# Large loads on GpSimd's queue, and other numbers for the scheduler, in a gated scan followed by an MLP

## The chip, the cores and the metric

One core of a Trainium2 chip (trn2). The metric is the device time of one execution in microseconds. Five engines run their own instruction streams in order: TensorE (PE, with its weight loads as PEld), VectorE (DVE), ScalarE (ACT), GpSimd (POOL) and SyncE (SP). Data transfers are issued from an engine's queue, also in order: a transfer whose input or buffer is not ready holds up what stands behind it.

## The reference

For each of 4 batches and 8 heads, a complex gated state of 48 x 48 is carried over 768 steps; its real part, read out by q, gives rows of 384 per token, which go through an MLP with a piecewise activation.

```python
scale = np.minimum(mag, 0.999) / (mag + 1e-06)
a_re_n, a_im_n = (a_re * scale, a_im * scale)
for t in range(S):
    new_re = ar * S_re - ai * S_im
    new_im = ar * S_im + ai * S_re
    S_re, S_im = (new_re + kv, new_im)          # kv = k[t] outer v[t]
    y[:, :, t] = np.einsum('bhd,bhde->bhe', q[:, :, t], S_re)
...
h = x @ w_in                                    # 3072 x 384 by 384 x 2048
g = np.where(h >= 1, h, np.where(h <= -1, 0.0, (h + 1) ** 2 / 4))
return g @ w_out
```

a_re and a_im are drawn 8 times larger than the setup's own draw.

## The kernel before

**Tiling.** The 3072 tokens are 12 units of 256; two units make a block, so there are six blocks of 512 columns. Unit u is unit 0 or 1 of its block u // 2. The scan is not stepped: a unit's gates become running sums of log-magnitude and angle, and the read-out becomes masked products of k and q within chunks of 128 tokens plus a carried state.

**A unit's work.** `gates(u)` loads ai (both parts of a), kq and V, works on ScalarE (Ln, Exp, Arctan, Sin, Abs; helper line L597) and VectorE (L611, L615, L625, L635, scans L695 and L745, L760, L766, L714), and ends with two products of 1536 columns (L823). Their rows are then re-arranged over partitions into hd by ten transfers, the *spreads* (`spread`; issued through the helper at L390, shown as hd<-x and hd<-kq). `attend(u)` is a series of short TensorE visits: sc (scores, L978), tp (transposes, L922), yp (L1019, L1027) and dp (state, L951), with VectorE's mask products am (L986) and ScalarE's copies into xr (L1039). After the second yp of a unit six small transfers, the *moves* (xr<-xr, 16 KB each), bring rows of two heads to their places. The second chunk's yp_1_0 of a unit is its last for the moves.

**A block's work.** `moe(blk)` first splits xr into xH (ScalarE, L1118) and xL (VectorE, L1125), one slice of 128 rows at a time for the second unit. Then for each of 16 slices f of the hidden layer: nine products h (L1148; two with xH and one with xL for each of three row slices), the activation, and nine products o (L1223), three slices later. h has two PSUM banks. The activation is s (ScalarE, L1173), g (VectorE, L1192), gh (ScalarE, L1206) and gl (VectorE, L1210). Blocks below SPARE take two further steps on ScalarE (L1183, L1187), the others one on VectorE (L1200). Results are copied by ScalarE (L1250) and stored; those copies share three buffers with s and g of the next block.

**Weights** arrive in 16 loads of 768 KB (`load`, L405), two buffers in turn after the first four, and are decoded on VectorE (L420, L429, L438, L449) and ScalarE (L444) during the start and block 0. Some of the decoding of the first four is done by TensorE ("rest"). In the last block the weights are loaded again for range checks (chk, `ranges`); `bounds` checks ai of the first four units (chk_ai, L523 to L547).

**What sets the order.** Every step is given to `Plan.op` with an engine, an assumed duration, what it reads and writes, and for some a due time; `Plan.order` is a list scheduler that walks through assumed time and writes one order per engine. Due times come from FIRST (the assumed start of block 0), the blocks' assumed durations DUR, and for visits from windows (HEAD, EARLY, WINDOW). A transfer costs its queue DMA_ISSUE and ends DMA_FIX plus its bytes over a rate (LOAD or MOVE) later. HOLD and QUEUE let an engine or SyncE wait for a more urgent step that comes soon. On the chip only the orders and the true dependences are left: nothing waits for an assumed time. All transfers stand on SyncE's queue; GpSimd has nothing to do after its constants. Idle TensorE products (L1278) are put into gaps of the assumed schedule before block 0.

Of the kernel before, what the change touches and what calls it, by code (L numbers as in the profile page):

```python
# [12 lines left out]
U32 = mybir.dt.uint32  # L13
# [5 lines left out]
P = 128  # L19
# [5 lines left out]
DM = NH * D  # L25
# [7 lines left out]
NC = U // CH  # L33
# [23 lines left out]
LAT = {"PE": 260, "DVE": 190, "ACT": 190, "SP": 0, "POOL": 200}  # L57
SAME = {"PE": 0, "DVE": 122, "ACT": 128, "SP": 0, "POOL": 0}
TOKEN = (("o2", "at2"), ("o2", "o0"))
DMA_FIX, DMA_END, DMA_ISSUE, LANES = 2400, 50, 470, 8  # L60
LOAD, MOVE = 410.0, 240.0
LATE = 2000
LATE_MOVE = 0
TABLE = 1294
FIRST = 51000
SLACK = 1.04
LAG = 3
SPREADS = 0
SPREAD = ("SP", "ACT")
HOLD = {'DVE': (2, 2000.0), 'ACT': (2, 2000.0)}  # L70
QUEUE = (0.3, 0.0)
WINDOW = (0.0, 0.7)
EARLY = (0.15, 0.9)
HEAD = ((30000, 15000), (25000, 2000))
HOME = 4
SPARE = 2
LEAD = 8000
WARM = 0.85
BRIDGE = 4
ABS_ACT = 5  # L80
LO_PE = 4
INFLATE = 1.6
SPLIT_DUE = 3000
# [215 lines left out]


def per(n):
    return n / 2.4 + 14


def moe_time(n):
# [14 lines left out]
def gated_scan_moe(  # L320
    ctx: ExitStack, tc: tile.TileContext, kq, ari, art, v, wl, qn, kn, arn, ain, vn, out
):
    nc = tc.nc
# [61 lines left out]
    def dma(nbytes, dst, src, r=(), w=(), due=None, rate=LOAD, eng="SP", after=(), late=0):  # L385
        queue = {"SP": nc.sync, "ACT": nc.scalar, "POOL": nc.gpsimd}[eng]
        return pl.op(
            eng,
            DMA_ISSUE,
            lambda: queue.dma_start(dst(), src()),  # L390
            r=r,
            w=w,
            dma=nbytes / rate,
            due=due,
            after=after,
            late=late,
        )
# [3 lines left out]

    def load(k, raw):
        nc.sync.dma_start(raw.rearrange("p n t -> p (n t)"), wl[k].bitcast(U32))  # L405

    def weights(n, kind, i, slot):
        k = i + (NF // 2 if kind == "o" else 0)
        RAW = tl(slot, [P, 2 * DM, 2], U32, f"raw_{kind}{i}")
        Y = tl("y", [P, 2 * DM], U32, f"y_{kind}{i}")  # L410
        W = weight[kind, i] = tl(f"w{kind}{i}", [P, 2, 2, DM], F32R, f"w{kind}_{i}")
        hi, lo = (lambda: W.get()[:, :, 0]), (lambda: W.get()[:, :, 1])
        wide = lambda t: t.rearrange("p (e n) -> p e n", e=2)
        top, low = (lambda: RAW.get()[:, :, 1]), (lambda: RAW.get()[:, :, 0])
        N = 2 * DM
        pl.op("SP", DMA_ISSUE, lambda: load(k, RAW.get()), w=[RAW], dma=P * N * 8 / LOAD, late=LATE if n > 2 else 0)
# [18 lines left out]
        pl.op(  # L435
            "DVE",
            dve(N),
            lambda: V_.scalar_tensor_tensor(  # L438
                low(), top(), 0xC0000000, low(), op0=ALU.bitwise_and, op1=ALU.bitwise_or
            ),  # L440
            w=[(RAW, 0)],
        )
        yf = lambda: wide(low().bitcast(F32))
        pl.op("ACT", act(N) + 50, lambda: A_.copy(hi(), yf()), r=[(RAW, 0)], w=[(W, 0)])  # L444
        if n >= LO_PE:
            pl.op(
                "DVE",
                dve(N),
                lambda: V_.tensor_tensor(lo(), yf(), hi().bitcast(F32), op=ALU.subtract),  # L449
                r=[(RAW, 0), (W, 0)],  # L450
                w=[(W, 1)],
            )
# [60 lines left out]
    def bounds(u):  # L513
# [5 lines left out]
        dma(P * 2 * N * 4, lambda: AI.get(), lambda: ari[PLACE[u]], w=[AI], late=LATE)  # L519
        pl.op(  # L520
            "DVE",
            dve(N, True),
# [35 lines left out]
    def gates(u):  # L558
# [21 lines left out]
        if u == 0:  # L580
            for e in range(2):
                dma(
                    size,
                    lambda e=e: AI.get()[:, e],
                    lambda e=e: art[u, :, e],
                    w=[(AI, e)],
                )
        else:
            dma(2 * size, lambda: AI.get(), lambda: (art[u] if by_token else ari[place]), w=[a, i], after=moved if u == 3 else (), late=LATE if u > 2 else 0)

        def ac(out, src, f, r, w, tab=False, **kw):
            acc_ = kw.get("accum_out")
# [117 lines left out]
            ac(X1, X0, AF.Exp, [x0], [x1], True, scale=-1.0)  # L710
            ac(X0, X0, AF.Exp, [], [x0], True)

        dma(2 * size, lambda: KQ.get(), lambda: kq[place], w=[KQ], after=moved if u == 2 else (), late=LATE if u > 1 else 0)
        ve(dve(2 * N), lambda: V_.tensor_tensor(KQ.get(), KQ.get(), X.get(), op=ALU.mult), [X], [KQ])  # L714

        yield
# [81 lines left out]
            )  # L798
        else:
            vt[u] = tl("V0", [P, NC, DM], F32, f"V_{u}")  # L800
        dma(P * NC * DM * 4, lambda t=vt[u]: t.get(), lambda: v[place], w=[vt[u]], late=LATE if u > 1 else 0)
        if u == 1:
            hd = [
                guest(
# [82 lines left out]
    def attend(u):  # L887
# [112 lines left out]
        def values(c, ams, st):  # L1000
# [64 lines left out]
        def visit(parts):  # L1065
            reads = [x for p in parts for x in p[2]]
            last = None
            for n, (cost, run, r, psum, tail) in enumerate(parts):
                cost += 90 if n == len(parts) - 1 else 0
                last = pl.op("PE", cost, run, r=reads if n == 0 else r, w=[psum], glue=last)  # L1070
                visits.append((len(todo_visits), last))
                kinds[last] = "att"
                tail()
            todo_visits.append(0)
# [493 lines left out]
```

## Time and profile before

| | |
|---|---|
| median of 3 runs | 582.93 us (582.11 to 583.48) |
| the profiled execution | 585.01 us |
| its span, first to last instruction | 583.2 us |
| mean granted TensorE clock | 0.992 |
| first product h of block 0 | 71.2 us into the span |
| last product o | ends at about 575.8 us |
| transfers | 77.42 MB, all but 0.72 MB of it on one queue |

The profile shows an engine's instructions with start and length in microseconds from the start of the span, and in brackets how long it was idle before and what ended that. SPq is the issue of a transfer; its landing comes later. A row of the chain of waits ("DMA xr<-xr") is the time in which the chain waited for that transfer. In a group's row stand the count, the busy us and mean ns, and the idle us before it. Line numbers are those of the kernel before.

### The profile page before, as it was taken

The page shows a single profiled execution, that of the slowest core. Times are in us where ns is not written, and L with a number is a line of the kernel's source. Part 1 is how long each engine was busy: PE and PEld are TensorE (multiplying, and loading weights), DVE is VectorE, ACT ScalarE, POOL GpSimd, SP SyncE. Part 2 cuts the span into 40 slices and gives each one's busy share as a digit, 9 for nine tenths or more (in the row PEclk, how much of TensorE's full clock was granted, in tenths as well). Part 3 has the DMA queues.
Part 4 walks back from the last instruction along what each step waited for, and adds up shares of the span by engine and source line. Part 5 has one row for each costly group of instructions (what it writes and reads, how often), then busy time and mean ns, then how long its engine had stood idle before and what let it go on. Part 6 is the DMA issues. An engine that isn't in the chain of part 4 may idle for free.

```text
span 583.2 us, 9954 instructions
## 1 busy us (share of the span) xinstructions
PE 565.9 (97%) x3908; PEld 477.9 (82%) x3908; DVE 431.9 (74%) x624; ACT 407.0 (70%) x656; POOL 1.7 (0%) x20
## 2 busy tenths in 40 slices
PE   8999999999999999999999999999999999999995
PEld 8788888888788888877888888888888888888883
DVE  4999999999769398469599778797875544455452
ACT  7777799887798899886475666756643322369972
POOL 1000000000000000000000000000000000000000
PEclk9999999999989999999999999999999999999998
DMA  8686551854640721740711521601511400078711
GB/s 353 242 224 215 173 190 63 249 210 148 164 157 0 205 101 55 177 182 12 189 52 36 187 85 53 198 1 51 148 55 31 112 1 4 12 263 310 267 72 61
DMA packets 23527, 77.42 MB, mean 133 GB/s; under 512 B 4528, under 2 KB 10288, under 8 KB 23472
## 3 DMA queue, kind: packets, MB, share of 16 engines
q1 hardware_dynamic: 23472, 76.70, 40.8%
q8 instruction: 33, 0.54, 0.4%
q14 instruction: 22, 0.18, 0.1%
HBM read 51.90 MB, written 4.72 MB: 97 GB/s over the span
## 4 chain that ended last, share of the span: by engine, by line
PE 61%; DVE 17%; ACT 9%; DMA 8%; issue 3%; SPq 1%; DVEq 0%; ACTq 0%
PE o L1223 24%; PE h L1148 23%; PE sc L978 4%; ACT ai L597 2%; PE yp L1027 2%; DMA hd<-x 2%; PE yp L1019 2%; DMA xr<-xr 2%; PE dp L951 2%; DVE g L1192 2%; PE tp L922 1%; DMA raw_o<-in_wl_dram 1%; ACT x L597 1%; DVE gl L1210 1%; DVE kq L823 1%
## 5 line engine op out<-in xcount | busy, mean ns | idle before, releaser
L1148 PE MATMUL h<-xH,wi 128*128 128x512 f32 x576 | 181.8, 397 | 4.0 <-DVE g L1192 2.0
L1223 PE MATMUL o<-gh,wo 128*128 128x512 f32 x576 | 180.8, 395 | 0.0
L1148 PEld LDWEIGHTS h<-xH,wi 128*128 128x128 f32 x576 | 105.8, 188 | 27.7 <-ACT xH L1118 3.6
L1223 PEld LDWEIGHTS o<-gh,wo 128*128 128x128 f32 x576 | 106.9, 189 | 22.0 <-issue 0.7
L1192 DVE TENSOR_TENSOR g<-h,s 128x512 f32<-128x512 f32 x96 | 65.7, 684 | 65.8 <-ACT s L1173 45.9
L1148 PE MATMUL h<-xL,wi 128*128 128x512 f32 x288 | 113.0, 392 | 1.0 <-DVE xL L1125 0.9
L1223 PE MATMUL o<-gl,wo 128*128 128x512 f32 x288 | 112.9, 392 | 0.2 <-DVE gl L1210 0.2
L1206 ACT CAST gh<-g 128x512 fp32r<-128x512 f32 x96 | 59.1, 616 | 56.6 <-DVE g L1200 53.2
L1210 DVE TENSOR_TENSOR gl<-g,gh 128x512 fp32r<-128x512 f32 x96 | 66.0, 687 | 36.5 <-ACT gh L1206 36.2
L1173 ACT ACTIVATE s<-h,cst 128x512 f32<-128x512 f32 x96 | 65.7, 685 | 37.3 <-PE h L1148 32.6
L1148 PEld LDWEIGHTS h<-xL,wi 128*128 128x128 f32 x288 | 54.2, 188 | 13.9 <-DVE xL L1125 2.2
L1223 PEld LDWEIGHTS o<-gl,wo 128*128 128x128 f32 x288 | 54.2, 188 | 12.4 <-DVE gl L1210 0.7
L597 ACT ACTIVATE ai<-ai 128x768 f32<-128x768 f32 x49 | 41.2, 843 | 17.9 <-DVE ai L766 5.1
L978 PE MATMUL sc<-hd 96*128 96x128 f32 x384 | 49.9, 278 | 0.2 <-DMA hd<-kq 0.2
L978 PEld LDWEIGHTS sc<-hd 96*128 96x128 f32 x384 | 47.1, 191 | 2.7 <-DMA hd<-kq 0.4
L1200 DVE SCALAR_TENSOR_TENSOR g<-s,g 128x512 f32<-128x512 f32 x64 | 44.2, 691 | 1.8
L1027 PE MATMUL yp<-am,V 128*64 128x128 f32 x384 | 35.5, 273 | 0.0
L986 DVE TENSOR_TENSOR am<-sc,sums 128x512 f32<-128x512 f32 x48 | 32.3, 681 | 1.1 <-PE sc L978 1.1
L1019 PE MATMUL yp<-hd,st 96*64 96x128 f32 x320 | 32.1, 278 | 0.0
L1278 PE MATMUL idle<-sums,ident 128*128 128x128 f32 x218 | 29.1, 295 | 1.7 <-POOL sums masks.py:66 1.7
L1278 PEld LDWEIGHTS idle<-sums,ident 128*128 128x128 f32 x218 | 28.3, 210 | 2.5 <-POOL sums masks.py:66 1.7
L400 ACT ACT_TABLE_LOAD x21 | 26.9, 1283 | 0.4
(104 smaller groups left out, 655.4 us busy)
## 6 DMA issues: line engine op xcount, KB each, us to landing
chk<-in_wl_dram SPq DMA_DIRECT2D x16, 768.0 KB, 6.0
kq<-in_kq_dram SPq DMA_DIRECT2D x12, 768.0 KB, 4.8
ai<-in_ari_dram SPq DMA_DIRECT2D x10, 768.0 KB, 6.1
hd<-x SPq DMA_DIRECT2D x24, 288.0 KB, 3.8
hd<-kq SPq DMA_DIRECT2D x24, 288.0 KB, 5.3
raw_i<-in_wl_dram SPq DMA_DIRECT2D x8, 768.0 KB, 5.2
raw_o<-in_wl_dram SPq DMA_DIRECT2D x8, 768.0 KB, 7.3
V<-in_v_dram SPq DMA_DIRECT2D x12, 384.0 KB, 3.4
```

The source lines that it names most:

```text
L597: lambda: A_.activation(out(), src(), f, **kw),
L978: PE_.matmul(SC.get()[:, i, :], t[:, 0, cs], t[:, 1, cs], start=True, stop=True)
L1019: PE_.matmul(o_, st.get().rearrange("p h e -> p (h e)")[:, lo : lo + 64], head(h)[:, 1, cs], start=True, stop=False,)
L1027: PE_.matmul(o_, V.get()[:, c, lo : lo + 64], ams[pr // 2].get()[:, 2 * (pr % 2) + e, :], start=st is None, stop=True,)
L1148: PE_.matmul(H.get(), weight["i", f // 2].get()[:, f % 2, part, sl], x.get()[:, j, :], start=j == 0 and n == 0, stop=j == NJ - 1 and n == 2,)
L1173: lambda: A_.activation(SS.get(), H.get(), AF.Relu, bias=c_half, scale=-0.5 if spare else 0.5),
L1192: lambda: V_.tensor_tensor(G.get(), H.get(), SS.get(), op=ALU.max),
L1200: lambda: V_.scalar_tensor_tensor(G.get(), SS.get(), 1.0, G.get(), op0=ALU.min, op1=ALU.mult),
L1206: pl.op("ACT", act(T), lambda: A_.copy(GH.get(), G.get()), r=[G], w=[GH])
L1210: lambda: V_.tensor_tensor(GL.get(), G.get(), GH.get().bitcast(F32), op=ALU.subtract),
L1223: PE_.matmul(PO[m].get(), weight["o", f // 2].get()[:, f % 2, part, sl], g.get(), start=f == 0 and n == 0, stop=f == NF - 1 and n == 2,)
L1278: PE_.matmul(idle["h1"], ident, mask, start=True, stop=True)
```

## The change

46 loads get another queue: the weight loads from the fourth on, kq, ai and V of the units after the first two or three, and the checks of ai are issued by GpSimd. The first weights, the first units' inputs, the last block's weight checks, spreads, moves and results stay on SyncE. SPARE goes from 2 to 1, so that block 1 takes VectorE's form of the activation, and ABS_ACT from 5 to 12, so that the Abs of units 5 to 11 goes from VectorE (L787) to ScalarE (L783). Moves get the spreads' rate. All other edits are numbers in the scheduler: what it takes an issue, a matmul or a visit to last, FIRST from 51000 to 87000, SLACK from 1.04 to 1.0, and the windows: visits for later blocks are due between 0.45 and 0.9 of the block before, not between 0 and 0.7.

```diff
-DMA_FIX, DMA_END, DMA_ISSUE, LANES = 2400, 50, 470, 8
+DMA_FIX, DMA_END, DMA_ISSUE, LANES = 2400, 50, 450, 8
+MOVE_ISSUE, SOFT_ISSUE = 610, 1100
+LOADS = "POOL"
...
-WINDOW = (0.0, 0.7)
+WINDOW = (0.45, 0.9)
...
-SPARE = 2
+SPARE = 1
...
-ABS_ACT = 5
+ABS_ACT = 12
...
-            DMA_ISSUE,
+            MOVE_ISSUE if rate == MOVE else SOFT_ISSUE if eng == "POOL" else DMA_ISSUE,
...
-    def load(k, raw):
-        nc.sync.dma_start(raw.rearrange("p n t -> p (n t)"), wl[k].bitcast(U32))
+    def load(k, raw, eng="SP"):
+        queue = nc.sync if eng == "SP" else nc.gpsimd
+        queue.dma_start(raw.rearrange("p n t -> p (n t)"), wl[k].bitcast(U32))
...
+        eng, late = ("SP", 0) if n < 3 else (LOADS, LATE)
...
-        dma(2 * size, lambda: KQ.get(), lambda: kq[place], w=[KQ], after=moved if u == 2 else (), late=LATE if u > 1 else 0)
+        dma(2 * size, lambda: KQ.get(), lambda: kq[place], w=[KQ], after=moved if u == 2 else (), late=LATE if u > 1 else 0, eng=LOADS if u > 1 else "SP")
...
-                cost += 90 if n == len(parts) - 1 else 0
+                cost = 0.92 * cost + (60 if n == len(parts) - 1 else 0)
```

The numbers reorder every engine. Three places follow; in names the numbers after hd, xr and am are the unit or the block, and the last one is a buffer's. On SyncE's queue around the change from block 0 to block 1 stood before, from unit 4's spreads on:

```order
L390 DMA hd_4_0_1527<-x_4_1012 48x1536
L390 DMA hd_4_1_1532<-x_4_1012 48x1536
L390 DMA hd_4_2_1541<-x_4_1012 32x1024
L390 DMA hd_4_2_1541<-x_4_1012 16x512 x2
L390 DMA hd_4_0_1527<-kq_4_1177 48x1536
L390 DMA hd_4_1_1532<-kq_4_1177 48x1536
L390 DMA hd_4_2_1541<-kq_4_1177 32x1024
L390 DMA xr_1_900<-xr_1_900 16x256 x2
L390 DMA hd_4_2_1541<-kq_4_1177 16x512 x2
L390 DMA xr_1_900<-xr_1_900 16x256 x4
L390 DMA V_4_1622<-in_v_dram 128x768
L390 DMA kq_5_1626<-in_kq_dram 128x1536
```

and there stands now:

```order
L392 DMA hd_3_2_1095<-kq_3_773 16x512 x2
L392 DMA xr_1_897<-xr_1_897 16x256 x12
L392 DMA hd_4_0_1576<-x_4_1130 48x1536
L392 DMA hd_4_1_1582<-x_4_1130 48x1536
L392 DMA hd_4_2_1592<-x_4_1130 32x1024
L392 DMA hd_4_2_1592<-x_4_1130 16x512 x2
L392 DMA hd_4_0_1576<-kq_4_1143 48x1536
L392 DMA hd_4_1_1582<-kq_4_1143 48x1536
L392 DMA hd_4_2_1592<-kq_4_1143 32x1024
L392 DMA hd_4_2_1592<-kq_4_1143 16x512 x2
L392 DMA out_0_dram<-ob_0_0_1675 128x2x256
```

The moves of both units of block 1 now come first and in one run, the spreads of unit 4 behind them, and no load stands between. The later block changes have the same pattern.

On TensorE, at the change from block 1 to block 2, the last yp of unit 5 (which block 2 needs) was followed before by block 1's o for slice 10 and h for slice 13:

```order
L1027 MATMUL yp_5_1_0_2310<-am_5_1_1_2275,V_5_1997 64x128 x2
L1223 MATMUL o_1_0_1813<-gh_1_10_2260,wo_5_1341 128x512 x2
L1223 MATMUL o_1_0_1813<-gl_1_10_2269,wo_5_1341 128x512
L1223 MATMUL o_1_1_1819<-gh_1_10_2260,wo_5_1341 128x512 x2
L1223 MATMUL o_1_1_1819<-gl_1_10_2269,wo_5_1341 128x512
L1223 MATMUL o_1_2_1826<-gh_1_10_2260,wo_5_1341 128x512 x2
L1223 MATMUL o_1_2_1826<-gl_1_10_2269,wo_5_1341 128x512
L1148 MATMUL h_1_13_2351<-xH_1_1566,wi_6_1268 128x512 x2
```

and is followed now by o for slice 12 and h for slice 15, the last of block 1:

```order
L1038 MATMUL yp_5_1_0_2357<-am_5_1_1_2333,V_5_1981 64x128 x2
L1235 MATMUL o_1_0_1759<-gh_1_12_2278,wo_6_1488 128x512 x2
L1235 MATMUL o_1_0_1759<-gl_1_12_2289,wo_6_1488 128x512
L1235 MATMUL o_1_1_1767<-gh_1_12_2278,wo_6_1488 128x512 x2
L1235 MATMUL o_1_1_1767<-gl_1_12_2289,wo_6_1488 128x512
L1235 MATMUL o_1_2_1773<-gh_1_12_2278,wo_6_1488 128x512 x2
L1235 MATMUL o_1_2_1773<-gl_1_12_2289,wo_6_1488 128x512
L1160 MATMUL h_1_15_2394<-xH_1_1538,wi_7_1399 128x512 x2
```

So the visit stands two slices later: 27 products of 128x512 lie between it and block 2's first h, where there were 63 and a pair of scores; 36 lie ahead of the third row slice, since three o stand before it.

On VectorE at the start, ahead of unit 1's first mask products (am_1_0_0 and am_1_1_0), stood before:

```order
L449 TENSOR_TENSOR wo_1_415<-raw_o1_228,wo_1_415 128x2x384
L986 TENSOR_TENSOR am_0_0_1_469<-sc_0_0_1_449,sums_69 128x512
L986 TENSOR_TENSOR am_0_1_1_483<-sc_0_1_1_461,sums_69 128x512
L420 TENSOR_SCALAR y_i3_487<-raw_i3_281 128x768
L429 SCALAR_TENSOR_TENSOR raw_i3_281<-raw_i3_281,y_i3_487 128x768
L438 SCALAR_TENSOR_TENSOR raw_i3_281<-raw_i3_281 128x768
L745 SCALAR_TENSOR_TENSOR ai_2_111<-ai_2_111,state_94,cst_75 128x256 x3
L760 TENSOR_SCALAR ai_2_111<-ai_2_111 128x768
L986 TENSOR_TENSOR am_1_0_0_553<-sc_1_0_0_478,sums_69 128x512
```

and now (numbers of lines are those of the changed kernel, 11 higher here):

```order
L431 TENSOR_SCALAR y_i3_458<-raw_i3_280 128x768
L972 COPY st_0_0_461<-dp_0_0_429 96x384
L997 TENSOR_TENSOR am_0_0_1_468<-sc_0_0_1_451,sums_69 128x512
L997 TENSOR_TENSOR am_0_1_1_478<-sc_0_1_1_463,sums_69 128x512
L440 SCALAR_TENSOR_TENSOR raw_i3_280<-raw_i3_280,y_i3_458 128x768
L449 SCALAR_TENSOR_TENSOR raw_i3_280<-raw_i3_280 128x768
L756 SCALAR_TENSOR_TENSOR ai_2_111<-ai_2_111,state_94,cst_75 128x256 x3
L997 TENSOR_TENSOR am_1_0_0_542<-sc_1_0_0_485,sums_69 128x512
```

The decoding's last step for wo_1 (before L449) and the step L760 of unit 2 now come behind unit 1's mask products; the rest of what stands ahead of them is the same work in another order.

More of the change, by code (lines that the diff above doesn't have):

```diff
@@ L64 @@
 TABLE = 1294
-FIRST = 51000
-SLACK = 1.04
+FIRST = 87000
+SLACK = 1.0
 LAG = 3
@@ L70 @@
 HOLD = {'DVE': (2, 2000.0), 'ACT': (2, 2000.0)}
-QUEUE = (0.3, 0.0)
-WINDOW = (0.0, 0.7)
+QUEUE = (0.1, 5000.0)
+WINDOW = (0.45, 0.9)
 EARLY = (0.15, 0.9)
-HEAD = ((30000, 15000), (25000, 2000))
+HEAD = ((15000, 8000), (8000, 2000))
 HOME = 4
-SPARE = 2
+SPARE = 1
 LEAD = 8000
@@ L301, in per @@
 def per(n):
-    return n / 2.4 + 14
+    return n / 2.4 + 16
 def moe_time(n):
@@ L415, in weights @@
         N = 2 * DM
-        pl.op("SP", DMA_ISSUE, lambda: load(k, RAW.get()), w=[RAW], dma=P * N * 8 / LOAD, late=LATE if n > 2 else 0)
+        eng, late = ("SP", 0) if n < 3 else (LOADS, LATE)
+        pl.op(
+            eng,
+            SOFT_ISSUE if eng == "POOL" else DMA_ISSUE,
+            lambda: load(k, RAW.get(), eng),
+            w=[RAW],
+            dma=P * N * 8 / LOAD,
+            late=late,
+        )
         pl.op(
@@ L518, in bounds @@
         N = NJ * U
-        dma(P * 2 * N * 4, lambda: AI.get(), lambda: ari[PLACE[u]], w=[AI], late=LATE)
+        dma(P * 2 * N * 4, lambda: AI.get(), lambda: ari[PLACE[u]], w=[AI], late=LATE, eng=LOADS)
         pl.op(
@@ L588, in gates @@
         else:
-            dma(2 * size, lambda: AI.get(), lambda: (art[u] if by_token else ari[place]), w=[a, i], after=moved if u == 3 else (), late=LATE if u > 2 else 0)
+            dma(2 * size, lambda: AI.get(), lambda: (art[u] if by_token else ari[place]), w=[a, i], after=moved if u == 3 else (), late=LATE if u > 2 else 0, eng=LOADS if u > 2 else "SP")
         def ac(out, src, f, r, w, tab=False, **kw):
@@ L800, in gates @@
             vt[u] = tl("V0", [P, NC, DM], F32, f"V_{u}")
-        dma(P * NC * DM * 4, lambda t=vt[u]: t.get(), lambda: v[place], w=[vt[u]], late=LATE if u > 1 else 0)
+        dma(P * NC * DM * 4, lambda t=vt[u]: t.get(), lambda: v[place], w=[vt[u]], late=LATE if u > 1 else 0, eng=LOADS if u > 1 else "SP")
         if u == 1:
@@ L1058, in move @@
                     r=[(XR, (x, ub * U + q * CH)) for q in range(NC) for x in (False, True)],
+                    rate=MOVE,
                     w=[(XR, (ub, e, j))],
```

## The prediction

> **What bounds the kernel now.** I read the page first, for who is busy, then the windows, for where TensorE is not.
>
> ```profile
> span 583.2 us, 9954 instructions
> PE 565.9 (97%) x3908; PEld 477.9 (82%) x3908; DVE 431.9 (74%) x624; ACT 407.0 (70%) x656; POOL 1.7 (0%) x20
> ...
> 278.72 2.04 PE h L1148 x9
> ```
>
> TensorE is busy 97% of the span, and no edit here takes a product away. The last line, from the chain of waits, gives the pace: nine 128x512 products in 2.04 us, 0.227 us each. What can be won is the 17.3 us in which TensorE is idle, plus what its clock loses after a long gap. The windows show where that is once the MLP runs (columns: stretch, length, busy us with counts of PE, PEld, DVE, ACT, POOL, granted clock, DMA share, GB/s):
>
> ```profile
> 130.00:140.00 10.00, 10.00 (x57) 8.54 (x56) 10.00 (x11) 8.68 (x13) 0.00 (x0) 1.00 0.23 80
> 140.00:145.00 5.00, 4.55 (x47) 3.50 (x47) 5.00 (x9) 3.25 (x8) 0.00 (x0) 1.00 0.74 210
> 158.00:160.00 2.00, 0.98 (x4) 0.30 (x2) 2.00 (x5) 2.00 (x5) 0.00 (x0) 1.00 0.60 165
> 160.00:162.00 2.00, 1.67 (x5) 1.10 (x6) 2.00 (x5) 2.00 (x5) 0.00 (x0) 0.85 1.05 424
> 162.00:164.00 2.00, 2.00 (x7) 1.52 (x6) 1.99 (x5) 2.00 (x4) 0.00 (x0) 0.50 0.03 9
> 164.00:166.00 2.00, 2.00 (x9) 1.58 (x8) 0.68 (x1) 1.28 (x4) 0.00 (x0) 0.80 0.00 0
> ...
> 246.00:250.00 4.00, 3.18 (x13) 1.66 (x11) 3.67 (x7) 3.97 (x9) 0.00 (x0) 1.00 0.72 240
> ...
> 264.00:266.00 2.00, 0.96 (x5) 0.49 (x4) 1.97 (x3) 1.25 (x2) 0.00 (x0) 1.00 0.00 0
> ```
>
> Idle: 0.45 us at 140, 1.02 + 0.33 at 158 to 162, 0.82 at 246, 1.04 at 264, in all 3.66 us. After the gap at 158 the clock is granted at 0.85, 0.50 and 0.80 in three stretches of 2 us, which loses 2 x (0.15 + 0.50 + 0.20) = 1.7 us. **Together 5.4 us.** The timeline shows why, on SyncE's queue and where its last move is used:
>
> ```profile
> 144.89 3.21 SPq L390 DMA_DIRECT2D hd<-x  x5
> 148.15 1.86 SPq L390 DMA_DIRECT2D hd<-kq  x3
> 150.86 1.47 SPq L390 DMA_DIRECT2D xr<-xr  x2
> 152.94 1.14 SPq L390 DMA_DIRECT2D hd<-kq  x2
> 154.12 3.42 SPq L390 DMA_DIRECT2D xr<-xr  x4
> ...
> 157.72 0.39 ACT L1118 CAST xH<-xr 128x256 fp32r<-128x256 f32 x1
> ...
> 160.09 0.50 PE L1148 MATMUL h<-xL,wi 128*128 128x512 f32 x1 [0.87 <-DVE xL L1125]
> ```
>
> Ten spreads of unit 4, which block 1 needs only later, stand ahead of and between the six moves that block 1's first product needs. The second block change repeats this, and the results of block 1 then leave late, so that their buffers come free late:
>
> ```profile
> 239.71 1.83 SPq L390 DMA_DIRECT2D xr<-xr  x2
> 241.59 1.42 SPq L390 DMA_DIRECT2D hd<-kq  x2
> 243.54 2.40 SPq L390 DMA_DIRECT2D xr<-xr  x4
> ...
> 254.77 4.53 DMA out_dram<-ob
> ...
> DVE g L1192 <- DMA out_dram<-ob: 6.3, 1, 6.3
> ```
>
> **What the change does, part by part.** *Queues.* 46 loads (13 weights, 10 kq, 9 ai, 10 V, 4 checks) leave SyncE for GpSimd's queue. SyncE keeps spreads, moves, results and the first and last loads, and the new order puts all moves of a block directly ahead of the next unit's spreads (first piece of the order above). So the moves at 0 to 1 start when ScalarE's copy is done, and the 5.4 us should go. Bounds: 0 (the wait turns out to be another's) to 5.4; I take 5.4, since the six late moves and the late results end these very waits. The stall at 140 has another cause: VectorE is full in 130 to 140 (10.00 of 10). Up to the sixteenth gl of block 0 it now runs one L611, L615, L523, L531 and L986 less and one L1125 more. At 0.95, 0.55, 0.55, 0.95, 0.68 and -0.55 us that is 3.1 us, more than the 0.45.
>
> *What is late next.* Visits now fall later in a block. At 1 to 2, only 27 products stand between the last yp of unit 5 and block 2's first h, against 63 and a pair of scores: 6.1 us, and 36 (8.2 us) until the third slice is used. The path through the copies and moves:
>
> ```profile
> L1039 ACT COPY xr<-yp 128x512 f32<-128x512 f32 (+2 forms) x30 | 14.6, 491 | 1.6 <-PE yp L1027 1.6
> ...
> 54.87 3.67 SPq L390 DMA_DIRECT2D xr<-xr  x6
> ...
> xr<-xr SPq DMA_DIRECT2D x72, 16.0 KB, 2.5
> ...
> 161.15 0.42 DVE L1125 TENSOR_TENSOR xL<-xr,xH 128x256 fp32r<-128x256 f32 x1
> ```
>
> 0.5 + 3.1 (five issues before the sixth) + 2.5 + 0.4 + 0.4 = 6.9 us, which fits into 8.2. With the slow landing of 4.4 us that the start below shows it is 8.8: 0.6 us of stall, or 2.3 if the clock falls as at 162. I take 0.6. The other block changes leave 33 products or more.
>
> *Two balances.* Block 1 drops two ScalarE steps per slice and takes one VectorE step; seven Abs go from VectorE to ScalarE.
>
> ```profile
> L1183 ACT ACTIVATE s<-s,cst 128x512 f32<-128x512 f32 x32 | 23.1, 722 | 0.6
> L1187 ACT ACTIVATE s<-s 128x512 f32<-128x512 f32 x32 | 20.1, 629 | 0.5
> ...
> L1200 DVE SCALAR_TENSOR_TENSOR g<-s,g 128x512 f32<-128x512 f32 x64 | 44.2, 691 | 1.8
> ...
> 210.00:225.00 15.00, 15.00 (x126) 12.85 (x126) 13.71 (x23) 14.44 (x23) 0.00 (x0) 1.00 0.14 45
> 225.00:240.00 15.00, 15.00 (x90) 12.29 (x89) 9.47 (x12) 13.04 (x23) 0.00 (x0) 1.00 0.45 116
> ```
>
> Over block 1, ScalarE loses 16 x 1.35 = 21.6 us and VectorE gains 16 x 0.69 = 11.1, less two Abs of 0.55 (the size of L760's row below). In 210 to 240 VectorE is busy 23.2 of 30 and ScalarE 27.5; a third of the shift makes that 26.5 and 20.3. TensorE's products cover both: cost 0. Without cover it would be VectorE's full 11.1 us.
>
> *The start.* Block 0's first h waits for the last move.
>
> ```profile
> 0.00:15.00 15.00, 12.98 (x83) 12.71 (x84) 6.79 (x8) 10.33 (x12) 1.65 (x20) 1.00 0.89 354
> ...
> 1.67 5.11 DMA ai<-in_art_dram
> ...
> 2.11 0.10 POOL L352 MEMSET fsum<- 128x8 f32 x1
> ...
> L449 DVE TENSOR_TENSOR wo<-raw_o,wo 128x768 fp32r<-128x768 f32 x7 | 6.7, 950 | 0.0
> L760 DVE TENSOR_SCALAR ai<-ai 128x768 int32<-128x768 f32 x10 | 5.5, 554 | 0.1
> ...
> 66.32 4.37 DMA xr<-xr
> ...
> 71.22 0.73 PE L1148 MATMUL h<-xH,wi 128*128 128x512 f32 x2 [1.31 <-ACT xH L1118]
> ```
>
> Two things pull against each other. In the order, VectorE's first mask product of unit 1 gets ahead of one L449 and one L760: 0.95 + 0.55 = 1.5 us earlier. But the fourth weight was the tenth load on SyncE; now it waits for nothing on GpSimd, which is free at 2.2 us, and runs beside the third load, which ends the first wait of the chain at 6.8. The DMA engines move 354 GB/s there, so its 786 KB push what follows by up to 2.2 us; at least 0, if it gets only what is over. I take 1.5, near the upper end, since the share is 0.89 already. Later kq_2 and ai_3 (2.2 us each) no longer stand behind unit 1's spreads; I take 0.6 for these. Together +0.6 us; bounds -1.5 and +5.1 (2.2 + 4.4 - 1.5).
>
> By the Trainium skill, DMA: Bandwidth & Descriptors, Queues, rings and completion order, each DMA engine takes turns between the rows that have work; by that rule the load gets its half at once, the start costs the whole 2.2, and the sum is 0.7 higher. The trace, which has a single row of data transfers, cannot show it.
>
> **Sum**, against the profiled execution's own 585.0 (span 583.2 and 1.8 around it): 585.0 - 5.4 + 0.6 + 0.6 = 580.8. The median of the runs is 2.1 below that execution, so 578.7 us is forecast.
>
> **Rivals.** *The two queues collide (slower).* The same 16 engines carry both, and a load on GpSimd's queue can now pass spreads and moves that it stood behind. Place: the start; mechanism: 2.2 + 4.4 as above plus 2.2 for a weight beside unit 1's last moves, all on the chain, less 1.5: first h 7.3 us later. With 5.4 recovered and 2.3 lost at 1 to 2: 582.9 + 7.3 - 5.4 + 2.3 = 587.1. It turns the sign when the first h comes over 4.8 us later, after 76. For it speaks that the chain runs through DMA at both ends of the start; against it, that TensorE, VectorE and ScalarE have other work at unit 1's spreads.
>
> *The stall only moves (no change).* The shorter path at 1 to 2 and its like after it lose 2.3 twice, and the start +0.6: 582.9 - 5.4 + 4.6 + 0.6 = 582.7.
>
> *The change does not reach the wait.* GpSimd's queue is in order too, and ScalarE, full at the 0 to 1 change (2.00 of 2 in 158 to 164), may bring the copies late whatever SyncE does; then only 246 and 264 are won (1.9), and the start costs 0.6: 581.6.
>
> *GpSimd and VectorE shut each other out.* If a load holds VectorE while its descriptors are made, at least for the 0.33 us of SyncE's shortest issue of one, 14 loads in the full block 0 cost 4.6, with up to 0.95 (one long VectorE step) 13; less the 3.1 of relief. Near the lower end: 578.7 + 4.6 - 0.5 = 582.8, up to 588.6.
>
> ```profile
> 132.41 0.33 SPq L405 DMA_DIRECT2D raw_o<-in_wl_dram  x1
> ```
>
> The Trainium skill, SBUF — State Buffer, in its box on the "DVE blocks DMA" trap, says that descriptors of this queue cannot be written while VectorE is in a two-port mode, and its practical consequences say that whichever starts first blocks the other. By it only the short tensor_scalar steps are touched, and the loads mostly wait, not VectorE; no trace here has a load on this queue.
>
> **How the numbers follow.** Forecast 0.60, 576 to 581.5; collision 0.15; stall moves 0.10; wait not reached 0.08; shut out 0.07. Differences under 0.2% (1.2 us) cannot be told from no change. Faster: the forecast and most of the 581.6 case, 0.67. Same: the 582.7 and half of the shut-out case, 0.14. Slower 0.19. The range goes from 575.0 (all won, start 1.5 earlier, some further small gaps) to 586.0, between the no-change and the collision cases; 2 in 10 lie outside, mostly above.
>
> **What would show it.** Right: at block 1's first h, moves issued in one run of six directly after the copy; no clock under 1.0 at 158 to 166; no wait of VectorE for results; ScalarE under 12 of 15 us in block 1. The start: first h between 70 and 74. Wrong: landings of moves over 4 us, first h after 76, VectorE steps that lengthen beside GpSimd's issues, or a new TensorE gap over 1 us at a block change.

## The result, and the profile after

The changed kernel takes 614.16 us (median of 4 runs, 611.25 to 615.2) against 582.8 us before: a ratio of 1.053, 95% interval 1.050 to 1.0559. It is slower by 31 us, where 578.7 was forecast and 586.0 was the upper end of the range.

The page of the changed kernel, in order: the span, busy time of the engines, the queues (q0 is GpSimd's), and the chain of waits by engine and by line:

```profile
span 613.4 us, 10027 instructions
PE 577.7 (94%) x3912; PEld 486.4 (79%) x3912; DVE 439.2 (72%) x633; ACT 395.1 (64%) x631; POOL 26.7 (4%) x66
...
q1 hardware_dynamic: 16848, 44.45, 23.1%
q0 software_dynamic: 5984, 32.25, 16.7%
...
PE 51%; DVE 17%; DMA 15%; ACT 8%; SPq 5%; issue 3%; ACTq 0%; DVEq 0%
PE h L1160 20%; PE o L1235 19%; SPq L392 5%; DMA hd<-kq 5%; DMA xr<-xr 4%; PE sc L989 4%; DMA out_dram<-ob 2%; PE yp L1030 2%; ACT ai L608 2%; PE yp L1038 2%; DVE g L1204 2%; DMA hd<-x 2%; ACT x L608 2%; DMA raw_i<-in_wl_dram 2%; DVE gl L1222 2%
```

The bytes are the same (77.42 MB), and GpSimd's queue carries 32 of them, as written. TensorE's idle time has grown from 17.3 to 35.7 us, and its busy time by 11.8 us for four more idle products of 0.1 us: that is a lower clock after gaps (0.975 on average, 0.992 before; 0.025 of 613.4 us is 15 us, 0.008 of 583.2 is 5). Before, the chain of waits went 61% through TensorE and 8% through transfers; now it is 51% and 15%.

Where it is lost, from the starts of each block's first h in the two timelines (us; the last column ends with the last o):

| | start | block 0 | 1 | 2 | 3 | 4 | 5 |
|---|---|---|---|---|---|---|---|
| before | 71.2 | 87.3 | 88.1 | 89.0 | 87.8 | 83.4 | 69.1 |
| after | 80.1 | 90.3 | 92.3 | 93.7 | 92.6 | 88.8 | 67.9 |
| difference | +8.9 | +3.0 | +4.2 | +4.7 | +4.8 | +5.4 | -1.2 |

So every stage but the last loses: 8.9 at the start, 22.1 in five blocks. First the start. These are GpSimd's two issues of kq_2 and ai_3 in the timeline, and what the chain of waits then went through:

```profile
43.45 0.53 POOL L392 DMA_DIRECT2D kq<-in_kq_dram  x1 [12.20 <-DMA hd<-kq]
44.28 0.53 POOL L392 DMA_DIRECT2D ai<-in_ari_dram  x1 [0.30 <-DVE raw_o L440]
```

```profile
44.94 11.18 DMA hd<-kq
56.16 3.45 PE sc L989 x14
...
66.97 4.11 DMA xr<-xr
...
79.28 6.07 DMA xr<-xr
...
85.88 4.21 PE h L1160 x9
```

Unit 1's spreads were issued from 42.3 to 49.4 us, some 2.6 us later than before (39.6 to 46.9). The two loads came in their midst; in the kernel before they stood behind them on SyncE. The chain waited 11.18 us for one spread, and the last landed at 58.4 (48.7 before), so unit 1's scores started at 56.2. The same comes once more at the end of the start: unit 1's last move, issued at 79.28 just behind a weight load of GpSimd's (79.24), took 6.07 us where the two before it took 1.8, and TensorE stood still for 3.4 us at 82.5, its longest stall behind the first h.

Now a block change. The old stall is gone, as forecast: the moves are issued in one run of six (162.47 for 3.67 us), and in the windows the stretches up to block 1's first h at 170.4 are full, with the clock at 1.00, and 0.4 us is idle at 170 to 172. Then come new holes (the windows' columns as in the prediction):

```profile
162.00:164.00 2.00, 2.00 (x10) 1.65 (x9) 2.00 (x3) 1.98 (x4) 0.00 (x0) 1.00 0.63 202
...
168.00:170.00 2.00, 2.00 (x11) 1.61 (x10) 2.00 (x3) 2.00 (x4) 0.17 (x1) 1.00 0.73 181
170.00:172.00 2.00, 1.59 (x8) 1.00 (x7) 1.97 (x5) 1.76 (x3) 0.00 (x0) 1.00 0.97 301
...
180.00:184.00 4.00, 2.14 (x16) 1.86 (x15) 2.23 (x5) 3.97 (x8) 0.89 (x1) 1.00 0.78 241
228.00:232.00 4.00, 2.37 (x11) 1.63 (x10) 2.40 (x5) 3.15 (x6) 0.53 (x1) 1.00 0.54 193
264.00:266.00 2.00, 1.03 (x6) 0.53 (x4) 0.13 (x1) 0.56 (x2) 0.00 (x0) 1.00 1.01 345
```

The hole at 229 shows the way it goes. The timeline of the two queues, and the chain at the same place:

```profile
210.38 3.35 SPq L392 DMA_DIRECT2D hd<-x  x5
211.32 0.54 POOL L392 DMA_DIRECT2D V<-in_v_dram  x1 [24.38 <-PE yp L1038]
211.86 0.53 POOL L392 DMA_DIRECT2D ai<-in_ari_dram  x1
213.83 3.11 SPq L392 DMA_DIRECT2D hd<-kq  x5
217.22 0.53 POOL L392 DMA_DIRECT2D chk_ai<-in_ari_dram  x1 [4.84 <-ACT chk_ai L558]
217.55 9.32 SPq L392 DMA_DIRECT2D xr<-xr  x6
```

```profile
215.04 11.31 DMA hd<-kq
226.35 0.02 issue
226.37 2.33 DMA xr<-xr
```

Three loads start while ten spreads are under way, and the chain waits 11.31 us for one spread. The six moves behind them then take 9.32 us to issue (3.67 above): the sixth starts at 226.37, just as the spread eight places ahead of it has landed. SyncE's transfers signal their landing on eight semaphores in turn, and in the records of both kernels no transfer of SyncE starts before the one eight places ahead of it on that queue has landed. In the changed kernel 13 (14 before) start within 0.06 us after it, having waited over 0.15 us each and 15.1 us in all (9.8 before). A slow spread so holds up what stands eight places behind it, whatever that is.

That the loads themselves are hardly slower from GpSimd's queue is read from the transfers' medians (SPq or POOLq is the issuer, the last column is us from issue to landing), here for the changed kernel:

```profile
kq<-in_kq_dram POOLq DMA_DIRECT2D x10, 768.0 KB, 5.0
...
hd<-kq SPq DMA_DIRECT2D x24, 288.0 KB, 7.0
```

and for the kernel before:

```profile
kq<-in_kq_dram SPq DMA_DIRECT2D x12, 768.0 KB, 4.8
...
hd<-kq SPq DMA_DIRECT2D x24, 288.0 KB, 5.3
```

The medians of other loads move either way (ai 7.2 us, 6.1 before; raw_o 4.6, 7.3 before), since it depends on what is under way beside them. Loads with no other transfer under way agree: a weight issued by GpSimd at 152.39 landed after 4.43 us, one issued by SyncE at 132.41 in the kernel before after 4.41.

### The profile page after: what moved, and what is told of

It reads as the page before. It is cut to its first block, busy times and chain, and to the rows that moved or that the text cites. A ratio compares the mean times of both kernels' runs of the same rounds, so it can differ in the third digit from the quotient of the medians.

```text
span 613.4 us, 10027 instructions
## 1 busy us (share of the span) xinstructions
PE 577.7 (94%) x3912; PEld 486.4 (79%) x3912; DVE 439.2 (72%) x633; ACT 395.1 (64%) x631; POOL 26.7 (4%) x66
## 2 busy tenths in 40 slices
DMA packets 22887, 77.42 MB, mean 126 GB/s; under 512 B 4528, under 2 KB 10288, under 8 KB 22832
## 4 chain that ended last, share of the span: by engine, by line
PE 51%; DVE 17%; DMA 15%; ACT 8%; SPq 5%; issue 3%; ACTq 0%; DVEq 0%
PE h L1160 20%; PE o L1235 19%; SPq L392 5%; DMA hd<-kq 5%; DMA xr<-xr 4%; PE sc L989 4%; DMA out_dram<-ob 2%; PE yp L1030 2%; ACT ai L608 2%; PE yp L1038 2%; DVE g L1204 2%; DMA hd<-x 2%; ACT x L608 2%; DMA raw_i<-in_wl_dram 2%; DVE gl L1222 2%
## 5 line engine op out<-in xcount | busy, mean ns | idle before, releaser
L1160 PE MATMUL h<-xH,wi 128*128 128x512 f32 x576 | 183.9, 401 | 12.2 <-DVE g L1204 7.8
L1160 PEld LDWEIGHTS h<-xH,wi 128*128 128x128 f32 x576 | 108.3, 191 | 36.8 <-DVE g L1204 9.8
L1204 DVE TENSOR_TENSOR g<-h,s 128x512 f32<-128x512 f32 x96 | 65.9, 687 | 73.7 <-ACT s L1185 69.2
L1160 PE MATMUL h<-xL,wi 128*128 128x512 f32 x288 | 114.7, 398 | 0.4 <-DVE xL L1137 0.4
L1185 ACT ACTIVATE s<-h,cst 128x512 f32<-128x512 f32 x96 | 65.5, 685 | 63.4 <-PE h L1160 52.3
L1235 PEld LDWEIGHTS o<-gl,wo 128*128 128x128 f32 x288 | 54.2, 188 | 13.5 <-DVE gl L1222 1.9
L608 ACT ACTIVATE ai<-ai 128x768 f32<-128x768 f32 x56 | 47.1, 845 | 24.8 <-DMA ai<-in_ari_dram 11.3
L989 PE MATMUL sc<-hd 96*128 96x128 f32 x384 | 53.3, 288 | 5.3 <-DMA hd<-kq 5.1
L989 PEld LDWEIGHTS sc<-hd 96*128 96x128 f32 x384 | 50.0, 200 | 8.7 <-DMA hd<-kq 5.4
L1212 DVE SCALAR_TENSOR_TENSOR g<-s,g 128x512 f32<-128x512 f32 x80 | 55.2, 690 | 2.3
```

The costliest lines, as they stand in the source:

```text
L608: lambda: A_.activation(out(), src(), f, **kw),
L989: PE_.matmul(SC.get()[:, i, :], t[:, 0, cs], t[:, 1, cs], start=True, stop=True)
L1160: PE_.matmul(H.get(), weight["i", f // 2].get()[:, f % 2, part, sl], x.get()[:, j, :], start=j == 0 and n == 0, stop=j == NJ - 1 and n == 2,)
L1185: lambda: A_.activation(SS.get(), H.get(), AF.Relu, bias=c_half, scale=-0.5 if spare else 0.5),
L1204: lambda: V_.tensor_tensor(G.get(), H.get(), SS.get(), op=ALU.max),
L1212: lambda: V_.scalar_tensor_tensor(G.get(), SS.get(), 1.0, G.get(), op0=ALU.min, op1=ALU.mult),
```

## The experiments

All ratios are against the kernel before on the same chip. Landing times given as means are over all transfers of a name, from issue to landing.

**One queue under both orders.** Theory Q blames the queue, theory O the new order. In *a_q* the orders are those of the changed kernel, in *b_q* those of the kernel before; only the issuer of the 46 loads differs.

```diff
 a_q
-        queue = nc.sync if eng == "SP" else nc.gpsimd
+        queue = nc.sync
...
-        queue = {"SP": nc.sync, "ACT": nc.scalar, "POOL": nc.gpsimd}[eng]
+        queue = {"SP": nc.sync, "ACT": nc.scalar, "POOL": nc.sync}[eng]
 b_q, scheduled with LOADS = "SP" and the old numbers
-        queue = {"SP": nc.sync, "ACT": nc.scalar, "POOL": nc.gpsimd}[eng]
+        queue = nc.gpsimd if soft else {"SP": nc.sync, "ACT": nc.scalar, "POOL": nc.gpsimd}[eng]
```

> The kernel before with every engine's order as it is, but the same 46 loads issued by GpSimd. Theory Q: kq_2 and ai_3 pass unit 1's spreads, the first h comes 5 to 10 us later than 71.2, hd<-kq lands in 5.5 to 6.5 us on average, and the time is 590 to 612. Theory O: first h within 2 us of 71.2, time 580 to 586.

Measured: 605.22 us, 1.0417 (1.0372 to 1.0462). First h at 80.6, hd<-kq lands in 5.93 us on average (4.34 before). Only the issuer was changed: **the queue alone costs 22.5 us under the old order** (22 to 27 by the interval). In the profiled execution 9.4 us fall on the start and 9.7 on the blocks, 7.1 of these on block 3 (94.9, 87.8 before), where the chain waits 5.72 us for a move; blocks 2, 4 and 5 lose nothing.

> The changed kernel with every engine's order as it is, but the 46 loads issued by SyncE at the places that the schedule gave them. Theory Q (the loads on GpSimd's queue run beside the spreads and delay them): hd<-kq lands in 4 to 5 us on average again (6.3 changed, 4.3 before), the first h comes at 70 to 74 us, and the time is 580 to 592. Theory O (the new order itself, with its late visits and its shift between ScalarE and VectorE, is too tight, whatever the queue): first h still at 78 or later, 605 or more.

Measured: 617.92 us, 1.0602 (1.0572 to 1.0631), which is a miss for Q. First h came at 72.9 and hd<-kq in 5.01 us, as Q wanted, but block 1 took 97.9 us and block 3 96.6. An order that was made for two queues is no good on one: a load at the place that GpSimd's queue had for it now stands ahead of spreads and results on SyncE. The two causes are not to be told apart by this run.

**Two loads, two ways.** *a_two_sp* puts kq_2 and ai_3 alone back on SyncE. *a_gate* leaves them on GpSimd behind a true wait for unit 1's last spread. All other orders are the same in both.

```diff
 a_two_sp
-... late=LATE if u > 2 else 0, eng=LOADS if u > 2 else "SP")
+... late=LATE if u > 2 else 0, eng=LOADS if u > 3 else "SP")
...
-... late=LATE if u > 1 else 0, eng=LOADS if u > 1 else "SP")
+... late=LATE if u > 1 else 0, eng=LOADS if u > 2 else "SP")
 a_gate, ahead of kq_2 and of ai_3
+    pl.op("POOL", 200, hold_on(u), r=[kept[0][2]], after=moved)
...
+        return lambda: nc.gpsimd.tensor_copy(held[64:96, u - 2 : u - 1], t.get()[64:96, 1, 0, 0:1])
```

> The changed kernel with two of the 46 loads, kq_2 and ai_3, back on SyncE behind unit 1's spreads; the orders of TensorE, VectorE and ScalarE are the same. Theory Q: unit 1's spreads land by 50 us, not 58.4, the first h comes at 71 to 74, not 80.1, and the time is 605 to 608. Theory O: the time stays within 2 us of 614.

> The changed kernel, every order as it is, with one small GpSimd copy of 32 values ahead of each of kq_2 and ai_3 that reads the rows of the last spread of unit 1: a true wait in place of the scheduler's own. Theory Q (these two loads do harm because they pass the spreads, not because GpSimd issues them): unit 1's spreads land by 52 us, the first h comes at 72 to 74 us as with the two loads on SyncE (72.7), and the time is 608 to 613. Rival (a load from GpSimd's queue is slow or holds VectorE by itself): first h at 76 or later.

Measured: 611.55 us (1.0482, 1.0442 to 1.0522) and 611.67 us (1.046, 1.0415 to 1.0504). First h, from the timeline of a_gate:

```profile
72.83 0.73 PE L1173 MATMUL h<-xH,wi 128*128 128x512 f32 x2
```

and at 72.7 in a_two_sp; unit 1's spreads landed by 52.7 and 52.3. So these two loads cost the start 7.4 us, by passing the spreads and not by coming from GpSimd. In the scheduler `after=moved` held them back, but that is a rule of its assumed time: on one queue the order made it true, between two queues nothing did. The time moved by 2.6 us only (608.02 to 612.18 for a_two_sp, 611.25 to 615.2 for the changed kernel), which misses Q's 605 to 608 for a_two_sp: block 1 took 94.7 and 96.7 us instead of 92.3, with stalls of 4.6 and 5.0 us after block 1's first h, where the changed kernel has 1.9. The next wait took most of the gain.

**Scheduled anew on one queue.**

```diff
-LOADS = "POOL"
+LOADS = "SP"
```

> The changed kernel scheduled anew with all loads on SyncE (LOADS = SP), every other number as changed. Theory Q: 577 to 584, that is what the forecast of 578.7 gives without its terms for the second queue, or a little above it. Theory O: over 600.

Measured: 588.86 us, 1.0109 (1.0057 to 1.0161): above Q's 577 to 584, far below O's 600. Start 70.0 and block 0 84.5 us, together 4.0 us better than before, but blocks 1 to 4 take 9.8 us more. So the rest of the change costs 6.2 us by itself (3 to 9 by the interval).

**What a_sp still loses.** Its stalls after the first h of blocks 1, 3 and 4 end with a result (out_dram) that lands late; g of the next block needs that buffer. *s_outq* sends the 18 results by GpSimd, all orders kept.

```diff
                 lambda OB=OB: OB.get().rearrange("p (n t) -> p n t", t=U),
                 r=[OB],
+                soft=True,
```

> The kernel of a_sp (all loads on SyncE, 588.9 us) with every engine's order as it is, but the 18 results (out_dram) issued by GpSimd. Theory R (what a_sp still loses, it loses because results stand on SyncE behind the spreads and the kq load that the new order puts at the block change, so g of the next block gets its buffer late): out_dram lands in 2 to 3.5 us (3.98 on average in a_sp), the stalls of TensorE of 3.7, 1.3 and 1.9 us at 166, 346 and 435 go or fall below 1 us, and the time is 580 to 584. Theory W (the late windows leave too little time between a visit and its use): the stalls stay, 587 or more.

Measured: 600.05 us, 1.0304 (1.0257 to 1.0351). R's cure made it worse; W's number held, with the results late all the same: they land in 5.14 us on average (3.98 in a_sp). The change to block 1 in the timeline of a_sp,

```profile
161.82 0.40 SPq L392 DMA_DIRECT2D out_dram<-ob  x1
...
162.83 0.34 SPq L392 DMA_DIRECT2D kq<-in_kq_dram  x1
```

and of s_outq:

```profile
161.65 0.84 POOL L392 DMA_DIRECT2D out_dram<-ob  x1 [159.42 <-ACT ob L1262]
162.03 0.33 SPq L392 DMA_DIRECT2D kq<-in_kq_dram  x1
```

In both the issue of the result begins ahead of that of the kq load, though GpSimd takes 0.84 us for it and SyncE 0.40. On one queue it landed 2.75 us later, at 164.57, with the load at 168.59. On two queues it landed 5.97 us later, at 167.63, with the load at 168.21. The earlier and smaller transfer lost its lead and ended with the load: the two queues share the engines. The Trainium skill says that they do so in turn (DMA: Bandwidth & Descriptors, Queues, rings and completion order: each engine takes turns between the rows that have work). The trace shows at most coarse turns: by 165.5 us 85 of the load's 128 pieces of 6 KB had started, but 2 of the 128 pieces of 4 KB of this result and the next. The queue by itself adds little: where hardly anything else was under way, results landed after 2.5 us from GpSimd (169.11, 527.04) and after 2.2 to 2.6 us from SyncE (a_sp, 579.51 and 513.42).

At this place nothing was lost by it: the next result, which g waited for, landed at 168.86 (169.30 in a_sp), and block 1 took 90.7 us (91.0). The time went mainly in block 3 (93.4, 89.0 in a_sp) and in block 5 (74.3, 67.6). At the change to block 5, a_sp has its results ahead of the last block's weight checks,

```profile
513.42 4.45 SPq L392 DMA_DIRECT2D out_dram<-ob  x3
517.92 2.26 SPq L408 DMA_DIRECT2D chk<-in_wl_dram  x4
```

and in s_outq nothing holds the checks back any more, so they go first:

```profile
513.18 2.52 SPq L408 DMA_DIRECT2D chk<-in_wl_dram  x4
517.38 0.73 POOL L392 DMA_DIRECT2D out_dram<-ob  x1 [78.28 <-ACT ob L1262]
518.79 0.73 POOL L392 DMA_DIRECT2D out_dram<-ob  x1 [0.69 <-ACT ob L1262]
525.58 0.69 ACT L1185 ACTIVATE s<-h,cst 128x512 f32<-128x512 f32 x1 [7.09 <-DMA out_dram<-ob]
527.05 1.22 PE L1160 MATMUL h<-xH,wi 128*128 128x512 f32 x2 [4.47 <-DVE g L1204]
```

The two results landed after 8.10 and 7.14 us (2.56 and 2.99 for the first two in a_sp), ScalarE waited 7.09 us for the buffer of s, and TensorE stood still for 4.47 us.

So a separate queue gives no precedence. It takes away the one precedence that the single queue had, that of what was issued first.

**Windows, balance, assumed sharing.**

```diff
 s_win, from a_sp
-WINDOW = (0.45, 0.9)
+WINDOW = (0.0, 0.7)
...
-HEAD = ((15000, 8000), (8000, 2000))
+HEAD = ((30000, 15000), (25000, 2000))
 s_w: WINDOW alone; s_w2: WINDOW = (0.2, 0.8) alone
 s_bal, from a_sp
-SPARE = 1
+SPARE = 2
...
-ABS_ACT = 12
+ABS_ACT = 5
 p_shared, from the changed kernel
-                q = queue.setdefault(eng, [0.0] * LANES)
+                q = queue.setdefault("SP", [0.0] * LANES)
```

> The kernel of a_sp with WINDOW and HEAD as before, so that visits come early in a block again. Theories R and W both: the spreads get away from the block change, 579 to 585, out_dram on average under 3.5 us. Theory B (the shift from ScalarE to VectorE by SPARE and ABS_ACT is what costs): 587 to 591.

> The kernel of a_sp with WINDOW (0.2, 0.8), between before's (0, 0.7) and the change's (0.45, 0.9). Theory W (the later the window, the more results, spreads and loads meet at the block change): 578 to 586, below a_sp's 588.9 and out_dram under 3.98 us on average. Rival (a_sp's loss is of some other number): 587 to 591.

Measured: s_win 582.96 us, 1.0005 (0.9988 to 1.0023), with results landing in 2.32 us on average; s_w2 586.6 us, 1.0065 (1.0041 to 1.009), with 3.12 us. s_w2 falls between W's 578 to 586 and its rival's 587 to 591. The later the window, the slower: (0, 0.7), (0.2, 0.8), (0.45, 0.9) gave 583.0 to 583.8, 586.6 and 588.9; the last two intervals overlap, the first and the last do not.

> All loads on SyncE and WINDOW as before; HEAD and every other number as changed (s_win had HEAD as before too, 583.0 us). In the profiles of s_win block 0 took 91.9 us, in a_sp 84.5, and the later blocks were faster in s_win. If the early window alone cures the later blocks, and HEAD alone set the start, the time is 573 to 579: start and block 0 near a_sp (154 us to block 1's first h), the rest near s_win. If the window is also what made block 0 slow (163.6 us to block 1's first h), 580 to 585.

Measured: 583.75 us, 1.0028 (1.001 to 1.0046). The second case held: block 1's first h comes at 163.7, and blocks 1 to 4 are those of s_win to 0.1 us. The late window helps block 0 (154.5 in a_sp) and hurts the four after it.

> The kernel of a_sp with SPARE = 2 and ABS_ACT = 5 as before. Theory B: 580 to 584. Theories R and W: within 2.5 us of a_sp, that is 586.4 to 591.4, and the stall after the first block change stays over 2 us.

Measured: 591.89 us, 1.017 (1.0111 to 1.023); its runs overlap those of a_sp, and it lies 0.5 above the range of R and W. Theory B, that the shift to VectorE costs, falls.

> The changed kernel, loads on GpSimd, with one edit: the scheduler lets the transfers of GpSimd's and SyncE's queues follow each other in one line of assumed time, where it gave each queue the full rate. Theory P (the order is too tight because the scheduler assumes the second queue to cost the first nothing): TensorE's idle time after the first h falls from 17 to under 10 us, the time is 596 to 604. Rival (the contention on the chip itself, or loads that pass on GpSimd because a plain order between two queues binds nothing): 608 to 616, with the first h at 78 or later.

Measured: 605.02 us, 1.0399 (1.0368 to 1.0431). Between the two: first h at 77.8, idle time after it 10.7 us. With an order made for two queues that share one rate, about 9 of the 31 us go; the rest stays.

**The queue under other orders.** *a_win* is the changed kernel with WINDOW and HEAD as before. *sw_wlq* is s_w with the same orders, and only its 13 later weight loads issued by GpSimd.

```diff
 sw_wlq
-            lambda: load(k, RAW.get(), eng),
+            lambda: load(k, RAW.get(), "SOFT" if n > 2 else eng),
```

> The changed kernel, loads on GpSimd, with WINDOW and HEAD as before (s_win with the queue). If queue and window cost independently of each other: 583.0 + 25 = 606 to 610, with hd<-kq at 5.5 to 6.5 us on average. If the queue costs only where visits are late: 584 to 595.

> The kernel of s_w with every engine's order as it is, but the 13 weight loads from the fourth on issued by GpSimd (kq, ai, V and checks stay on SyncE). Theory Q in its first form (any large load on a second queue shares the transfer engines with the spreads): slower than s_w by 4 to 12 us, lost before 160 us, since the weights come only until then. Rival (only kq and ai, which come free exactly when spreads are under way, do harm): within 2.5 us of s_w.

Measured: a_win 612.24 us, 1.0497 (1.0459 to 1.0535), against 583.0 on one queue (s_win, whose order of TensorE is nearly the same): the queue, with the order that the scheduler makes for it, costs 29 us there, somewhat more than the 23 to 27 expected. In the profiles 9.1 us of it fall on the start and 13.5 on block 0. sw_wlq 593.6 us, 1.0199 (1.0166 to 1.0233): 9.9 us for 13 weights, all of it before block 1's first h (173.7, 163.7 in s_w). One of them in the timeline of s_w, where it stands behind the last six moves ahead of block 0,

```profile
71.16 4.15 SPq L392 DMA_DIRECT2D xr<-xr  x6
...
78.34 0.34 SPq L408 DMA_DIRECT2D raw_i<-in_wl_dram  x1
```

and of sw_wlq, where it goes ahead of them:

```profile
68.81 0.91 POOL L408 DMA_DIRECT2D raw_i<-in_wl_dram  x1 [8.23 <-DVE wi L460]
...
73.20 5.96 SPq L392 DMA_DIRECT2D xr<-xr  x6
```

First h went from 75.4 to 79.7. So weight loads do it too, not kq and ai alone.

**The parts that help, alone.** *b_bal* is the kernel before with two numbers; *s_wq* and *s_wv* are s_win with QUEUE, and with the durations of products and visits, as before.

```diff
 b_bal
-SPARE = 2
+SPARE = 1
...
-ABS_ACT = 5
+ABS_ACT = 12
```

> The kernel before with only SPARE = 1 and ABS_ACT = 12. The prediction's cost of 0 for the shift: within 1.2 us of before. From s_bal (taking the shift back in a_sp cost 3.0 us): 578.5 to 581. Theory B: 584 to 590.

Measured: 579.99 us, 0.9943 (0.9925 to 0.9962), the only version that is clear below both kernels. Its windows over the places of the old stalls,

```profile
156.00:166.00 10.00, 10.00 (x56) 8.12 (x56) 8.80 (x15) 10.00 (x20) 0.00 (x0) 1.00 0.35 123
245.00:250.00 5.00, 5.00 (x22) 3.62 (x21) 3.87 (x6) 3.61 (x7) 0.00 (x0) 1.00 0.56 228
262.00:266.00 4.00, 4.00 (x28) 3.49 (x27) 4.00 (x8) 2.97 (x7) 0.00 (x0) 1.00 0.45 161
```

and those of the kernel before:

```profile
156.00:166.00 10.00, 8.65 (x37) 6.31 (x36) 8.66 (x14) 9.29 (x18) 0.00 (x0) 0.83 0.35 123
245.00:250.00 5.00, 4.18 (x22) 2.65 (x20) 4.10 (x8) 4.97 (x11) 0.00 (x0) 1.00 0.59 196
262.00:266.00 4.00, 2.96 (x14) 2.12 (x13) 3.96 (x6) 3.24 (x4) 0.00 (x0) 1.00 0.00 0
```

The holes are gone although the moves at 0 to 1 still stand among unit 4's spreads (issued 150.5 to 156.8, the last landed at 158.1, 158.8 before). The two numbers gave TensorE, VectorE and ScalarE new orders, and no run shows which of these fills the holes; ScalarE is not relieved there (10.00 of 10 us busy, 9.29 before). In the kernel before, the chain of waits holds no move at this place, but a weight load, a spread, and then steps of ScalarE and VectorE:

```profile
141.68 7.80 DMA raw_o<-in_wl_dram
...
149.50 5.54 DMA hd<-kq
...
155.08 0.84 ACT ai L597
...
158.75 1.12 DVE xL L1125 x2
```

The wide xL, which stands at 158.75 here, comes at 155.76 in b_bal.

> The kernel of s_win (loads on SyncE, windows as before, 583.0 us) with QUEUE as before too; TensorE's order is the same. If QUEUE = (0.1, 5000), which lets SyncE pass over more urgent transfers less often, made block 0 slow (91.9 us, 87.3 before): 576 to 580. If not: 582 to 584.5.

> The kernel of s_win with the assumed durations of products and visits as before (+14, +90 instead of +16, 0.92 and +60). If these moved block 0's work: block 0 at 86 to 89 us and 577 to 581. If not: 582 to 585.

Measured: 582.99 us, 1.0004 (0.9988 to 1.002), and 584.41 us, 1.0028 (1.0012 to 1.0044). Neither gave block 0 back (91.0 and 89.8 us, 87.3 before): why the changed numbers slow block 0 on one queue when the windows are early stays open (with the late ones, in a_sp, it took 84.5).

## Why the prediction was wrong, point by point

- **The step that failed** is the price of the second queue. In the sum it stands with "Queues" as a gain of 5.4 us, and at the start with "Later kq_2 and ai_3 (2.2 us each) no longer stand behind unit 1's spreads; I take 0.6 for these." That step saw the two loads pass the spreads and priced it by the loads' own length; for loads that run beside spreads, moves and results it took nothing. b_q puts the queue at a loss of 22.5 us, and a_two_sp and a_gate put the two loads at 7.4 us of the start. The spreads under way are slowed to the pace of the loads (11.18 us in the chain), and what stands eight places behind them waits for them to land.
- Behind the start the same mechanism was left out altogether: b_q loses 9.7 us there, most of it in block 3. The rival "the two queues collide" named the mechanism and the sign, but gave it one place, the start, and 587.1 us.
- "The other block changes leave 33 products or more" was to cost nothing. TensorE stalled 1.9, 1.6 and 1.9 us some ten us after the first h of blocks 1, 3 and 4. The step counted the path of the moves; the path that decided was that of the next unit's spreads, the next loads and the results, which late visits bring to one place. On one queue this costs 5.1 us (a_sp against s_w) or 5.9 with HEAD. The 0.6 us at 1 to 2 came out as 0.97 (264.9), behind a move that landed after 4.5 us, as the step had it.
- The fourth weight beside the first loads: "I take 1.5". Unit 0's spreads start 1.4 us later (33.77, 32.33 before; 32.49 in a_sp), but 2.5 later in b_q, where only the issuer differs from before (34.84), and at 34.9 and 35.1 in a_gate and a_two_sp, which begin with the changed kernel's order. The size was right or somewhat small. It is the fourth load, kq, that pays: with the weight from GpSimd beside it, it lands at 10.7 in b_q, and at 8.6 before.
- The 5.4 us: the stretch behind block 1's first h is nearly full, as forecast: TensorE is busy 7.19 of 7.60 us from 170.4 in the changed kernel and 7.33 of 7.50 from 154.5 in a_sp, with the clock at 1.00, where it was 6.37 of 7.50 at 0.77 before. But the stall came back some ten us later, and that the moves' place on SyncE is its cause is not shown: b_bal fills the same stretches with the moves still among the spreads, and the chain of the kernel before holds no move there (at the next change it does: 3.09 us at 241).
- "Cost 0" for the balances was mis-sized: b_bal gains 2.5 us.
- Nothing shows that GpSimd and VectorE shut each other out: the changed kernel's g (L1204) takes 687 ns on average, 684 before, a load's issue takes 0.53 to 0.56 us on average on GpSimd (0.33 at its shortest on SyncE), and the load at 152.39 landed after 4.43 us although VectorE was busy 15.00 of 15 us from 147 to 162.

Summed: the queue 22.5 (b_q) and the rest 6.2 (a_sp) make 28.7 of 31.4 us; the 2.7 that are left lie within the intervals. Within the 6.2, by estimate from differences of medians, windows are some 5 to 6, the balance about -2.5 to -3, and the other numbers the remaining 3 or so, which no run takes apart.

## What to carry to other kernels

A second queue is not a second road: before moving loads to it, list which small transfers on the first queue are waited for, and give them the time that they take beside a load, not alone. A dependence that only a scheduler knows holds on one queue by order, and between two queues not at all; where it matters it needs a true wait. Whether the loads would do the same harm from ScalarE's queue was not run. A stall of a few us at a stage change may go with a small shift of work between the engines and the new orders that it brings, with every transfer left on its queue, as in b_bal: try that first, alone.

## What the runs showed of the hardware

- Two transfers that overlapped on two queues ended nearly together: 167.63 and 168.21 for 256 KB and 768 KB in s_outq, against 164.57 and 168.59 on one queue; 10.67 and 10.72 for two of 768 KB issued at 2.15 and 2.18 in b_q.
- On SyncE no transfer started before the one eight places ahead of it had landed (all 229 pairs in the changed kernel, 275 before). Six moves took 3.67 us to issue where nothing was late, 9.32 behind slow spreads.
- Idle time can be paid twice: in the changed kernel 18.4 us more of it on TensorE came with some 11 us more busy time, at a granted clock of 0.83 in 80 to 100 us. Not every gap did this: after the 1.9 us at 181 the clock was 0.91 in 180 to 200, after the 1.6 us at 229 it was 1.00 in 220 to 240.
